# Rows of two scratch tensors in DRAM widened to multiples of 64 bytes: token list places of 64 bytes, x rows of 1600 bytes

## Chip, cores and metric

One core of a Trainium2 chip runs the whole kernel. The metric is the device time of one execution in microseconds (us). The output is one float32 tensor of 3072 x 384.

## What is computed

A delta-rule attention, then a router that sends each token to one of 8 experts, then that expert's two matrix products:

```python
# attention: B, H, S, D = 4, 8, 768, 48, all float32
k_n = k / (norm(k) + 1e-06)
for t in range(S):
    y[:, :, t] = q[:, :, t] @ state
    v_old = state^T k_n[:, :, t]
    state = state + beta[t] * outer(k_n[:, :, t], v[:, :, t] - v_old)
# bridge: x is y as 3072 tokens (N = B*S) of 384 numbers (H*D)
logits = cosine(x, expert_emb) / tau          # 8 experts
expert_idx = argmax(logits); gate_w = softmax(logits)[expert_idx]
for e in range(E):
    mask = expert_idx == e
    h = relu(x[mask] @ w1[e])                 # 384 -> 1024
    out[mask] = gate_w[mask] * (h @ w2[e])    # 1024 -> 384
```

## The kernel before

**Attention.** The sequence is cut into 12 chunks of 64 steps, and a *unit* is one chunk of two of the four batches, so there are 24 units, taken in order. A unit is loaded by SP (`load`, L112 to L127: q, k and v, rows of 192 bytes), prepared on POOL and VectorE (`prep1` to `prep3`, L294 to L310), and goes through a chain of small matrix products on TensorE (L286 is the helper `mm` that issues nearly all of them) with evictions on ScalarE and VectorE. `PLAN` (L568) gives every step of a unit a place in time; the steps of all units are sorted by it, and that order is what PE, DVE, ACT and POOL run. SP's DMAs are placed by the scheduler.

**Lists of tokens.** `outputs` (L441) writes a unit's rows of x into an SBUF tile `xc`, which holds two chunks of all four batches (256 tokens in each half, 4 units). After each second chunk, that is after every fourth unit and six times in all, the steps `route1` to `route6` (L481 to L539) pick each token's expert and its place in that expert's list. `put_on_lists` (L544) then issues four indirect DMAs from POOL (L551), called *puts* here: each scatters 128 token numbers to 128 places of `idmap`, a tensor in DRAM that has 3072 places for each of 8 experts and 3968 more behind them. Tokens of one expert get places that follow each other, so their numbers lie next to each other, 4 bytes each. `route6` writes the gate behind each row of x as its 385th number and stores the rows to `x_dram` in four DMAs by SP (L539), each of 64 partitions with two rows of 1540 bytes.

**Fill.** At the start `late_constants` (L217) fills `idmap` with the number N of a row of zeros: POOL makes a tile `none` (L254), SP stores it (L255), and SP stores the row of zeros to `x_dram` (L258).

**Experts.** From the counts of the lists 31 tiles of 128 places are laid out on one partition of VectorE (L609 to L631). `fetch` (L634) is called two tiles ahead; SP reads the expert and the place into registers, then reads the 128 places of `idmap` into `ids` (L638, only once all puts have landed), loads the expert's `w1` and `w2` (L642, L644; three buffers each), and POOL gathers the 128 rows of x by `ids` (L646). `transposed` (L651) transposes them on PE (L655), `experts` (L659) does the two products (L665, L670) and scales by the gate (L672), and POOL scatters 128 rows of 1536 bytes to the output (L673). At the start of this stage PE transposes the first two tiles before the first product.

The lines that tie the two scratch tensors together:

```python
    x_dram = tc.dram_tile([N + 1, Dm + 1], F32, name="x_dram")           # L76
    idmap = tc.dram_tile([NMAP, 1], I32, name="idmap")                   # L77
        none = ac.tile([128, NMAP // 128], I32, name="none")             # L253
        nc.gpsimd.iota(none, pattern=[[0, NMAP // 128]], base=N, channel_multiplier=0)
                out=idmap[:, :], out_offset=bass.IndirectOffsetOnAxis(ap=K["slot_i"][:, g:g + 1], axis=0),
                in_=K["tokid"][:, c - 1 + g // NU, g % NU:g % NU + 1], in_offset=None)
        ids = mk.tile([128, 1], I32, name="ids", tag="ids", bufs=5)      # L637
        read = nc.sync.dma_start(ids, idmap[bass.ds(s, T), :])           # L638
```

Of the kernel before, what the change touches and what calls it, by code (L numbers as in the profile page):

```python
# [8 lines left out]
F32 = mybir.dt.float32  # L9
I32 = mybir.dt.int32  # L10
# [12 lines left out]
def kernel(  # L23
# [37 lines left out]
    nc = tc.nc  # L61
    B, H, S, D = q.shape
    NC, NP, Dm, N = S // C, H // 2, H * D, B * S
    NU = B // 2
# [2 lines left out]
    NT = N // T + E - 1  # L67
    NMAP = E * N + NT * T

    cpool = ctx.enter_context(tc.tile_pool(name="const", bufs=1))  # L70
    att = ExitStack()
    ps = att.enter_context(tc.tile_pool(name="ps", bufs=1, space=bass.MemoryType.PSUM))
    run = cpool.tile([1, E], F32, name="run")
    base_e = cpool.tile([1, E], F32, name="base_e")
    K = {}
    x_dram = tc.dram_tile([N + 1, Dm + 1], F32, name="x_dram")  # L76
    idmap = tc.dram_tile([NMAP, 1], I32, name="idmap")  # L77

    def bank(shape):
        return ps.tile(shape, F32, name="bank", tag="bank", bufs=2)  # L80
# [15 lines left out]
    ac = att.enter_context(tc.tile_pool(name="ac", bufs=1))  # L96
    io = att.enter_context(tc.tile_pool(name="io", bufs=2))
# [35 lines left out]
    for u in range(NU):  # L133
        for i in range(2):
            nc.scalar.dma_start(out=bt[u * H:(u + 1) * H, :, i],
                                in_=beta[2 * u + i].rearrange("h (c t) -> h c t", t=C))
# [35 lines left out]
    def filled(name, bufs, value):  # L172

        ts = []
        for i in range(bufs):
            t = ac.tile(jc, F32, name=f"{name}{i}")
            nc.scalar.activation(t.rearrange("p j r c -> p (j r) c"), id64.broadcast_to(hc), ACT.Copy, scale=value)
            ts.append(t)
        return ts
# [28 lines left out]
    sqb = sqb.rearrange("p c (u h) -> p c u h", u=NU)  # L208

    PP = {s: filled(f"P{s}_", 2, 1.0) for s in LEVELS}  # L210
    S_u = []
    for u in range(NU):
        t = ac.tile([128, NP, 2, D], F32, name=f"S{u}")
# [3 lines left out]
    def late_constants():  # L217

        c = {}
        for name, value in (("second", ALU.is_ge), ("first", ALU.is_lt)):  # L220

            c[name] = ac.tile([128, 1], F32, name=name)
            nc.vector.tensor_single_scalar(c[name], trow_f[:, 0:1], float(C // 2), op=value)
        nc.vector.reciprocal(rtau, rtau)
        c["ones"] = ac.tile([128, 128], F32, name="ones")
        nc.vector.memset(c["ones"], 1.0)
        c["mask_su"] = ac.tile([128, 128], F32, name="mask_su")
        nc.gpsimd.memset(c["mask_su"], 1.0)
        nc.gpsimd.affine_select(out=c["mask_su"], in_=c["mask_su"], compare_op=ALU.is_ge, fill=0.0, base=-1,
                                pattern=[[1, 128]], channel_multiplier=-1)  # L230
        iota_ei = ac.tile([128, E], I32, name="iota_ei")
        nc.gpsimd.iota(iota_ei, pattern=[[1, E]], base=0, channel_multiplier=0)
        iota_e = ac.tile([128, E], F32, name="iota_e")
        nc.vector.tensor_copy(iota_e, iota_ei)
        c["pref_e"] = ac.tile([128, 1, E], F32, name="pref_e")
        nc.vector.tensor_scalar(c["pref_e"][:, 0, :], iota_e, -1.0, float(E), op0=ALU.mult, op1=ALU.add)
        nc.vector.tensor_scalar_mul(base_e, iota_e[0:1], float(N))
        nc.vector.tensor_copy(run, base_e)

        prow_f = ac.tile([128, 1], F32, name="prow_f")  # L240
        nc.vector.tensor_copy(prow_f, prow[:, 0:1])
        nc.vector.tensor_single_scalar(prow_f, prow_f, float(C), op=ALU.is_ge)
        nc.vector.scalar_tensor_tensor(out=prow_f, in0=prow_f, scalar=float(S), in1=trow_f[:, 0:1],
                                       op0=ALU.mult, op1=ALU.add)
        tok_i = ac.tile([128, NC, NU], I32, name="tok_i")
        nc.gpsimd.iota(tok_i, pattern=[[C, NC], [2 * S, NU]], base=0, channel_multiplier=0)
        tok_f = ac.tile([128, NC, NU], F32, name="tok_f")
        nc.vector.tensor_copy(tok_f, tok_i)
        nc.vector.tensor_scalar(tok_f, tok_f, prow_f, None, op0=ALU.add)
        c["tokid"] = ac.tile([128, NC, NU], I32, name="tokid")  # L250
        nc.vector.tensor_copy(c["tokid"], tok_f)

        none = ac.tile([128, NMAP // 128], I32, name="none")  # L253
        nc.gpsimd.iota(none, pattern=[[0, NMAP // 128]], base=N, channel_multiplier=0)  # L254
        nc.sync.dma_start(idmap.rearrange("(p n) o -> p (n o)", p=128), none)  # L255
        zrow = ac.tile([1, Dm + 1], F32, name="zrow")
        nc.vector.memset(zrow, 0.0)
        nc.sync.dma_start(x_dram[N:N + 1, :], zrow)  # L258
        K.update(c)
# [23 lines left out]
    outs = {}  # L283
# [80 lines left out]
    def product(lhsT, rhs):  # L364

        p = pair([NP, C])
        for j in range(NP):
            for a in range(2):
                for b in range(2):
                    mm(p[HALF[b], a, j], lhsT[HALF[a], j, b], rhs[HALF[a], j, b])  # L370
        return p.rearrange("p a j c -> p j a c")

    def level(U, s, by):
        p = product(U["A"][by], U["T"])
        U["P"] = PP[s][U["n"] % 2]
        nc.vector.copy_predicated(U["P"], below[s].broadcast_to(jc), p)  # L376
# [32 lines left out]
    def apply(lhsT, rhs):  # L409
        p = bank([128, H, D])  # L410
        for h in range(H):
            for i in range(2):
                mm(p[HALF[i], h], lhsT[HALF[i], h // 2, h % 2], rhs[HALF[i], h])
        return p
# [26 lines left out]
    def outputs(U):  # L441
        c, u = U["c"], U["u"]
        if u == 0 and c % 2 == 0:
            outs[c // 2] = (io.tile([128, 2, NU, Dm + 1], F32, name="xc", tag="xc"),
                            wk.tile([128, 2, NU], F32, name="ssx", tag="ssx"),
                            wk.tile([128, 2, NU, E], F32, name="lz", tag="lz"))
        xc, ssx, _ = outs[c // 2]
        p = apply(U["M"], U["Z"])
        U["x"] = xc[:, c % 2, u, 0:Dm]
        xh = U["x"].rearrange("p (h d) -> p h d", h=H)  # L450
        if c > 0:
            nc.vector.tensor_tensor(xh, p, U["Yq"], op=ALU.add)
        else:
            nc.vector.tensor_copy(xh, p)
        ysq = wk.tile([128, Dm], F32, name="ysq", tag="ysq", bufs=1)
        nc.scalar.activation(ysq, U["x"], ACT.Square, accum_out=ssx[:, c % 2, u:u + 1])
# [21 lines left out]
    def last_of_two_chunks(f):  # L478
        return lambda U: f(U["c"], *outs[U["c"] // 2]) if U["n"] % G == G - 1 else None
# [64 lines left out]
    def put_on_lists(g):  # L544

        def step(c, xc, ssx, lz):
            if g > 0:
                nc.gpsimd.memset(gap, 0.0)  # L550
            put = nc.gpsimd.indirect_dma_start(  # L551
                out=idmap[:, :], out_offset=bass.IndirectOffsetOnAxis(ap=K["slot_i"][:, g:g + 1], axis=0),
                in_=K["tokid"][:, c - 1 + g // NU, g % NU:g % NU + 1], in_offset=None)
            if g == 0:
                for other in lists[-G:]:
                    tc.add_manual_dep(put.ins, other.name, AFTER, reason="tokens' lists: two chunks after two others")
            else:
                tc.declare_no_dep(put.ins, group=f"lists{c}", reason="tokens' lists: distinct places")
            tc.add_to_no_dep_group(f"lists{c}", put.ins)
            lists.append(put.ins)  # L560
        return last_of_two_chunks(step)
# [31 lines left out]
    mk = ctx.enter_context(tc.tile_pool(name="mk", bufs=2))  # L593
# [40 lines left out]
    def fetch(i):  # L634
        e = nc.values_load(info[0:1, 0, i:i + 1], engines=(SP,), min_val=0, max_val=E - 1)
        s = nc.values_load(info[0:1, 1, i:i + 1], engines=(SP,), min_val=0, max_val=NMAP - T)
        ids = mk.tile([128, 1], I32, name="ids", tag="ids", bufs=5)  # L637
        read = nc.sync.dma_start(ids, idmap[bass.ds(s, T), :])  # L638
        for put in lists[-G:]:
            tc.add_manual_dep(read.ins, put.name, AFTER, reason="tokens' lists are complete")  # L640
        w1 = wt.tile([128, KC, F], F32, name="w1", tag="w1")
        nc.sync.dma_start(w1, moe_w1[bass.ds(e, 1)].rearrange("o (c p) f -> p (o c) f", p=128))  # L642
        w2 = wt.tile([128, NF, Dm], F32, name="w2", tag="w2")
        nc.sync.dma_start(w2, moe_w2[bass.ds(e, 1)].rearrange("o (f p) m -> p (o f) m", p=128))  # L644
        x = mk.tile([128, Dm + 1], F32, name="xg", tag="xg", bufs=5)
        nc.gpsimd.indirect_dma_start(  # L646
            out=x, out_offset=None, in_=x_dram[:, :],
            in_offset=bass.IndirectOffsetOnAxis(ap=ids[:, 0:1], axis=0))
        return ids, w1, w2, x
# [9 lines left out]
    def experts(xT, ids, w1, w2, x):  # L659
# [9 lines left out]
        for f in range(NF):  # L669
# [5 lines left out]
            in_=y, in_offset=None, bounds_check=N - 1, oob_is_err=False)  # L675

    ahead = [fetch(0), fetch(1)]
    xT = transposed(ahead[0][-1])
    for i in range(NT):
# [36 lines left out]
```

## Time and profile before

| | |
|---|---|
| three runs | 879.0, 879.75 (median), 882.95 us |
| the profiled execution | 880.7 us, of which the span of the trace is 879.0 |
| PE busy | 743.8 us (85%), 15196 instructions |
| DVE, ACT, POOL busy | 279.5, 245.3, 226.1 us |
| DMA queue of SP | 128738 packets, 116.55 MB, 46.8% of 16 engines |
| DMA queue of POOL (the indirect DMAs) | 4736 packets, 10.85 MB, 3.3% |
| instruction queue | 119 packets, 1.95 MB, 1.0% |
| granted TensorE clock, whole span | 0.94 of full speed |

All rows are from one execution; times are from the start of its span, on which the attention lies up to about 495 us, the layout of the tiles and the first fetches up to about 530, and the experts behind that. PEld is the weight load of TensorE. A bracket such as `[2.72 <-issue]` behind a row says how long the engine was idle before that row and what ended the wait; `issue` means that the engine waited for nothing that the profile shows. A "q" behind an engine's name (SPq) is its sequencer.

### The profile page before, as it was taken

How to read it: one execution, taken by the hardware profiler on the slowest of the kernel's cores; microseconds unless marked ns; L12 is line 12 of the kernel's file. 1: busy time of each engine (PE TensorE's matmuls, PEld its weight loads, DVE VectorE, ACT ScalarE, POOL GpSimd, SP SyncE). 2: the span in 40 equal slices, each digit the busy share in tenths (PEclk: the TensorE clock that was granted, in tenths of full speed). 3: DMA queues.
4: the chain of work that ended last, by engine and by line, in shares of the span. 5: the costliest groups of instructions: out<-in, count | busy, mean ns of one | idle time of the engine just before them, and what ended most of it. 6: DMA issues, size and time to landing. Idle time of an engine off the chain costs nothing. (4 is left out here: it accounts for less than half of the span.)

```text
span 879.0 us, 33263 instructions
## 1 busy us (share of the span) xinstructions
PE 743.8 (85%) x15196; PEld 636.6 (72%) x15196; DVE 279.5 (32%) x627; ACT 245.3 (28%) x468; POOL 226.1 (26%) x258
## 2 busy tenths in 40 slices
PE   1589899699789979979978308999999999999995
PEld 1478888588778868868867307777777777777774
DVE  5355556356445545534533300000000000010000
ACT  4155445254344535434523101111111111111110
POOL 3544234242423432342210201111111111111110
PEclk9999999899899999989978558999999999999998
DMA  4432112521611241040001369999999999999940
GB/s 86 77 58 56 34 35 38 56 53 35 66 31 36 50 60 33 13 48 4 4 3 40 35 242 363 329 324 321 327 326 315 328 328 328 309 323 317 329 140 0
DMA packets 134189, 129.63 MB, mean 147 GB/s; under 512 B 84538, under 2 KB 119521, under 8 KB 134050
## 3 DMA queue, kind: packets, MB, share of 16 engines
q1 hardware_dynamic: 128738, 116.55, 46.8%
q0 software_dynamic: 4736, 10.85, 3.3%
q8 instruction: 119, 1.95, 1.0%
q14 instruction: 20, 0.16, 0.1%
q10 hardware_dynamic: 576, 0.11, 0.1%
HBM read 117.91 MB, written 10.95 MB: 147 GB/s over the span
## 5 line engine op out<-in xcount | busy, mean ns | idle before, releaser
L665 PE MATMUL acc<-xTm,w 128*128 128x128 f32 x1488 | 172.9, 277 | 0.0
L665 PEld LDWEIGHTS acc<-xTm,w 128*128 128x128 f32 x1488 | 170.5, 194 | 0.3
L670 PE MATMUL acc<-w,hT 128*128 128x384 f32 x496 | 165.1, 486 | 0.0
L670 PEld LDWEIGHTS acc<-w,hT 128*128 128x128 f32 x496 | 91.9, 190 | 57.5
L667 ACT ACTIVATE hT<-acc 128x512 f32<-128x512 f32 x62 | 37.0, 597 | 331.0 <-PE acc L665 331.0
L672 DVE TENSOR_SCALAR y<-acc,xg 128x384 f32<-128x384 f32 x31 | 19.2, 618 | 305.0 <-PE acc L670 305.0
L673 POOL DMA_INDIRECT out_dram<-y,ids x31 | 31.6, 1018 | 270.1 <-DVE y L672 270.1
L286 PE MATMUL pair<-W,P 64*64 64x64 f32 x3072 | 78.5, 231 | 18.4 <-issue 14.1
L376 DVE COPY_PREDICATED P<-below,pair 128x512 f32<-128x512 int32 x96 | 70.7, 737 | 68.7 <-PE pair L286 54.4
L362 ACT ACTIVATE W<-pair 128x512 f32<-128x512 f32 x96 | 57.5, 599 | 111.2 <-PE pair L286 99.7
L301 POOL TENSOR_TENSOR rn<-rn,half 128x8 f32<-128x8 f32 x24 | 39.5, 1644 | 177.5 <-DVE rn L300 143.7
L286 PEld LDWEIGHTS pair<-W,P 64*64 64x64 f32 x3072 | 67.3, 143 | 22.6 <-issue 17.5
L286 PE MATMUL bank<-Z,G 64*64 64x48 f32 x1536 | 62.1, 232 | 13.4 <-issue 12.1
L286 PEld LDWEIGHTS bank<-Z,G 64*64 64x64 f32 x1536 | 57.0, 149 | 14.5 <-issue 12.3
L286 PE MATMUL bank<-R,W 64*64 64x48 f32 x1536 | 58.8, 225 | 8.5 <-issue 6.5
L286 PEld LDWEIGHTS bank<-R,W 64*64 64x64 f32 x1536 | 54.2, 142 | 10.1 <-issue 9.3
L286 PE MATMUL pair<-T,AJ 64*64 64x64 f32 x1536 | 42.9, 237 | 10.5 <-issue 7.7
L346 PE MATMUL bank<-ident,W 128*128 128x128 f32 x288 | 48.8, 293 | 1.2 <-ACT W L362 0.9
L655 PE MATMUL acc<-ident,xg 128*128 128x128 f32 x93 | 16.0, 283 | 35.0 <-DMA xg<-x_dram,ids 35.0
L655 PEld LDWEIGHTS acc<-ident,xg 128*128 128x128 f32 x93 | 12.3, 145 | 44.9 <-issue 31.7
L286 PEld LDWEIGHTS pair<-T,AJ 64*64 64x64 f32 x1536 | 34.9, 145 | 12.5 <-issue 8.9
L340 POOL TENSOR_TENSOR G<-G,upper 128x512 f32<-128x512 f32 x24 | 30.7, 1279 | 37.5 <-ACT G L334 36.1
(160 smaller groups left out, 881.5 us busy)
## 6 DMA issues: line engine op xcount, KB each, us to landing
w<-in_moe_w_dram SPq DMA_DIRECT2D x62, 1536.0 KB
x_dram<-xc SPq DMA_DIRECT2D x24, 192.5 KB
k_in<-in_k_dram SPq DMA_DIRECT2D x48, 96.0 KB
QQ<-in_q_dram SPq DMA_DIRECT2D x48, 96.0 KB
v_in<-in_v_dram SPq DMA_DIRECT2D x48, 96.0 KB
ids<-idmap SPq DMA_DIRECT2D x31, 0.5 KB
xg<-x_dram,ids POOLq DMA_INDIRECT x31
out_dram<-y,ids POOLq DMA_INDIRECT x31
```

What stands on the lines that cost most here:

```text
L286: nc.tensor.matmul(out_, lhsT=lhsT, rhs=rhs, start=start, stop=True, skip_group_check=True)
L301: nc.gpsimd.tensor_tensor(out=U["rn"], in0=U["rn"], in1=half[:, 0], op=ALU.pow)
L340: nc.gpsimd.tensor_tensor(M, M, upper.broadcast_to(hc), op=ALU.mult)
L346: nc.tensor.transpose(p[:, j].rearrange("p r c -> p (r c)"), src[:, j].rearrange("p r c -> p (r c)"), ident)
L362: nc.scalar.activation(out_, in_, ACT.Copy)
L376: nc.vector.copy_predicated(U["P"], below[s].broadcast_to(jc), p)
L655: nc.tensor.transpose(psX[:, j, :], x[:, j * 128:(j + 1) * 128], ident)
L665: nc.tensor.matmul(psH[:, i, :], lhsT=w1[:, j, (f + i) * 128:(f + i + 1) * 128], rhs=xT[:, j, :], start=(j == 0), stop=(j == KC - 1))
L667: nc.scalar.activation(hT[:, f:f + 4, :], psH, ACT.Relu)
L670: nc.tensor.matmul(psO, lhsT=hT[:, f, :], rhs=w2[:, f, :], start=(f == 0), stop=(f == NF - 1))
L672: nc.vector.tensor_scalar_mul(y, psO, x[:, Dm:Dm + 1])
L673: nc.gpsimd.indirect_dma_start(out=out[:, :], out_offset=bass.IndirectOffsetOnAxis(ap=ids[:, 0:1], axis=0), in_=y, in_offset=None, bounds_ ...
```

## The change

A place of `idmap` becomes 16 numbers, 64 bytes, and a put writes 16 copies of the token's number to it; `tokid` holds the copies, and the fill and the reads of `ids` carry 16 times the bytes. A row of `x_dram` becomes 400 numbers, 1600 bytes (384 of x, the gate, 15 zeros). Since only the first 385 are written by the computation, the zeros are set once in two tiles `XC` that are used in turn in place of the pool's two buffers. The fill is made by a memset where it was an iota.

```diff
+    ROW, ID = Dm + 16, 16
...
-    x_dram = tc.dram_tile([N + 1, Dm + 1], F32, name="x_dram")
-    idmap = tc.dram_tile([NMAP, 1], I32, name="idmap")
+    x_dram = tc.dram_tile([N + 1, ROW], F32, name="x_dram")
+    idmap = tc.dram_tile([NMAP, ID], I32, name="idmap")
...
+    XC = []
+    for i in range(2):
+        XC.append(ac.tile([128, 2, NU, ROW], F32, name=f"XC{i}"))
+        nc.gpsimd.memset(XC[i][:, :, :, Dm:], 0.0)
...
-        c["tokid"] = ac.tile([128, NC, NU], I32, name="tokid")
-        nc.vector.tensor_copy(c["tokid"], tok_f)
-
-        none = ac.tile([128, NMAP // 128], I32, name="none")
-        nc.gpsimd.iota(none, pattern=[[0, NMAP // 128]], base=N, channel_multiplier=0)
+        c["tokid"] = ac.tile([128, NC, NU, ID], I32, name="tokid")
+        nc.vector.tensor_copy(c["tokid"], tok_f.unsqueeze(3).broadcast_to([128, NC, NU, ID]))
+
+        none = ac.tile([128, NMAP // 128 * ID], I32, name="none")
+        nc.gpsimd.memset(none, N)
         nc.sync.dma_start(idmap.rearrange("(p n) o -> p (n o)", p=128), none)
-        zrow = ac.tile([1, Dm + 1], F32, name="zrow")
+        zrow = ac.tile([1, ROW], F32, name="zrow")
...
-            outs[c // 2] = (io.tile([128, 2, NU, Dm + 1], F32, name="xc", tag="xc"),
+            outs[c // 2] = (XC[c // 2 % 2],
...
-                in_=K["tokid"][:, c - 1 + g // NU, g % NU:g % NU + 1], in_offset=None)
+                in_=K["tokid"][:, c - 1 + g // NU, g % NU], in_offset=None)
...
-        ids = mk.tile([128, 1], I32, name="ids", tag="ids", bufs=5)
+        ids = mk.tile([128, ID], I32, name="ids", tag="ids", bufs=5)
...
-        x = mk.tile([128, Dm + 1], F32, name="xg", tag="xg", bufs=5)
+        x = mk.tile([128, ROW], F32, name="xg", tag="xg", bufs=5)
```

The order of PE, DVE and ACT stays as it was. POOL has the two small memsets of `XC` more among its first ones, and an instruction of another size at the fill. This is POOL before, at the fill (`Ksq`, `rn` and `KK_109` prepare the second unit, `ess` belongs to the experts' embeddings):

```order
L246 IOTA tok_i 128x24
L254 IOTA none 128x223
L296 TENSOR_TENSOR Ksq<-k_in 128x384
L301 TENSOR_TENSOR rn<-rn,half 128x8
L310 TENSOR_TENSOR KK_109<-k_in,rn 128x8x48
L268 TENSOR_TENSOR ess<-ess,half 8x1
```

and this is POOL now, with everything in the same order behind a memset of 3568 numbers per partition:

```order
L252 IOTA tok_i 128x24
L260 MEMSET none 128x3568
L302 TENSOR_TENSOR Ksq<-k_in 128x384
L307 TENSOR_TENSOR rn<-rn,half 128x8
L316 TENSOR_TENSOR KK_109<-k_in,rn 128x8x48
L274 TENSOR_TENSOR ess<-ess,half 8x1
```

On SP, before, the fill stands between the two halves of the fourth unit's q:

```order
L116 DMA QQ_84<-in_q_dram 64x8x48
L255 DMA idmap<-none 128x223
L116 DMA QQ_84<-in_q_dram 64x8x48
L258 DMA x_dram<-zrow 1x385
L116 DMA v_in<-in_v_dram 64x8x48 x2
L116 DMA k_in<-in_k_dram 64x8x48 x2
```

and now it stands two DMAs later, behind the row of zeros, with the loads of the second unit's v and of the fifth unit's k right behind it:

```order
L118 DMA QQ_84<-in_q_dram 64x8x48 x2
L264 DMA x_dram<-zrow 1x400
L261 DMA idmap<-none 128x3568
L118 DMA v_in<-in_v_dram 64x8x48 x2
L118 DMA k_in<-in_k_dram 64x8x48 x2
```

## Rows read from the trace of the kernel before

**Rows 1.** Experts' stretch: length; busy (instructions) of PE, PEld, DVE, ACT, POOL; PEclk, DMA, GB/s.

```profile
556.00:860.00 304.00, 303.00 (x1869) 242.04 (x1869) 29.89 (x55) 33.44 (x56) 53.99 (x55) 1.00 0.91 307
```

**Rows 2.** The scatters to the output: the page's groups (busy, mean ns, idle before).

```profile
L673 POOL DMA_INDIRECT out_dram<-y,ids x31 | 31.6, 1018 | 270.1 <-DVE y L672 270.1
```

**Rows 3.** The same view, each stretch one unit, from one L423 to a next.

```profile
144.06:170.12 26.06, 17.38 (x567) 15.47 (x569) 9.70 (x24) 9.50 (x18) 9.73 (x12) 0.91 0.53 56
170.12:186.71 16.59, 15.81 (x564) 14.51 (x561) 8.92 (x17) 8.22 (x16) 5.36 (x5) 0.94 0.20 40
186.71:203.27 16.56, 15.27 (x555) 13.74 (x545) 8.88 (x17) 8.21 (x16) 5.32 (x5) 1.00 0.20 40
203.27:221.58 18.31, 16.96 (x576) 15.47 (x578) 10.92 (x26) 8.22 (x16) 6.29 (x6) 1.00 0.19 37
221.58:247.60 26.02, 18.82 (x567) 17.45 (x563) 9.83 (x24) 8.22 (x17) 9.60 (x12) 0.80 0.53 56
...
297.61:320.63 23.02, 17.15 (x564) 15.47 (x560) 9.82 (x24) 8.55 (x17) 9.54 (x12) 0.93 0.47 63
...
371.91:397.12 25.21, 19.33 (x561) 17.56 (x557) 9.64 (x23) 8.40 (x17) 9.59 (x12) 0.80 0.36 42
```

**Rows 4.** Timeline around the first four puts: start, us, engine, line, operation, [idle before].

```profile
155.60 1.01 POOL L551 DMA_INDIRECT idmap<-tokid,slot_i  x1 [0.17 <-issue]
...
159.70 0.26 PE L286 MATMUL bank<-Z,G 64*64 64x48 f32 x3 [2.72 <-issue]
...
163.92 0.38 PE L286 MATMUL pair<-W,P 64*64 64x64 f32 x3 [1.68 <-issue]
167.22 0.51 PE L286 MATMUL pair<-W,P 64*64 64x64 f32 x6 [2.92 <-issue]
```

**Rows 5.** Timeline around the fifth four puts, after the last load of the attention.

```profile
450.86 0.96 POOL L551 DMA_INDIRECT idmap<-tokid,slot_i  x1 [0.22 <-issue]
...
454.84 0.22 PE L286 MATMUL bank<-enT,xT 128*64 128x8 f32 x1 [1.36 <-issue]
...
462.00 0.56 PE L286 MATMUL bank<-R,W 64*64 64x48 f32 x5 [4.50 <-issue]
```

**Rows 6.** By stretch: the end of that wait, and the four stores of x behind it.

```profile
457.50:462.00 4.50, 0.00 (x0) 0.00 (x0) 0.00 (x0) 0.00 (x0) 0.00 (x0) 0.50 0.00 0
...
464.00:468.50 4.50, 4.50 (x123) 4.05 (x117) 1.98 (x3) 1.02 (x2) 0.00 (x0) 0.50 0.72 183
```

**Rows 7.** Timeline, from the last put to the first read of a list.

```profile
499.69 0.96 POOL L551 DMA_INDIRECT idmap<-tokid,slot_i  x1 [0.22 <-issue]
...
511.38 0.39 SPq L638 DMA_DIRECT2D ids<-idmap  x1
```

**Rows 8.** SP's waits: us in total, times, longest.

```profile
SPq L638 <- DMA idmap<-tokid,slot_i: 7.7, 1, 7.7
```

**Rows 9.** SP's instructions of the line that reads the lists.

```profile
L638 SPq EVENT_SEMAPHORE  x35: 27/28/28, 510.7 to 827.8; - x35
L638 SPq ALU_OP  x31: 32/33/53, 502.9 to 827.7; - x31
```

**Rows 10.** POOL's groups up to 25 us: busy us, mean ns of one, idle before.

```profile
L214 POOL MEMSET S<- 128x384 f32 x2 | 0.8, 407 | 0.0
...
L254 POOL IOTA none<- 128x223 int32 x1 | 0.3, 333 | 0.0
...
L228 POOL MEMSET mask_su<- 128x128 f32 x1 | 0.2, 206 | 0.0
```

**Rows 11.** Timeline at the start: from the fill to the first unit's products.

```profile
19.70 0.33 POOL L254 IOTA none<- 128x223 int32 x1
...
20.01 0.82 POOL L296 TENSOR_TENSOR Ksq<-k_in 128x384 f32<-128x384 f32 x1
...
22.18 0.48 DVE L300 TENSOR_REDUCE rn<-Ksq 128x8 f32<-128x384 f32 x1
...
22.64 1.28 SPq L116 DMA_DIRECT2D v_in<-in_v_dram  x2
...
29.09 1.32 PE L286 MATMUL pair<-KT 48*64 48x128 f32 x17
...
46.40 0.83 POOL L314 TENSOR_TENSOR v_in<-v_in,sqb 128x384 f32<-128x384 f32 x1
```

## The prediction
> **What bounds the kernel now.** I read the table by stretches first, then the timeline at the places where a stretch is longer than its neighbours, then SP's waits at the seam between attention and experts. While the experts run, PE is busy in 303.00 of 304.00 us at the full clock [rows 1]; nothing that the change does to lists or rows of x is waited for there, so this part keeps its length and only its start can move. In the attention the work of one unit is some 560 matmuls. Three units in a row take 16.59, 16.56 and 18.31 us for 564, 555 and 576 of them, 17.15 in the mean, but every fourth unit takes 23 to 26 us for the same number [rows 3]. It is always the unit in which POOL issues four puts. What is lost there is in the timeline: PE stands still for 2.72, 1.68 and 2.92 us, and each of these waits is put down to "issue": no engine, no tile, no DMA of data that the profile shows [rows 4]. That looks like PE waiting for its own instructions, which come by DMA through the same 16 engines; the profile does not name it, so this stays an inference.
>
> What blocks the DMA engines is told by the fifth four puts, because there they are alone: no load of the attention is left, and the stores of x come later. Still PE stops for 1.36 and then 4.50 us [rows 5]. In the whole of the second stop every engine is idle and the DMA share is 0.00 [rows 6]: nothing is being moved, something is being waited out. It ends at 462.00, 11.1 us after the last of these puts was issued at 450.86. Around the first four puts the last stop ends at 167.22, 11.6 us after the last put, issued at 155.60 [rows 4]. And at the end of the attention SP, which waits for the puts by name, comes free at 510.7 [rows 9], 11.0 us after the last put at 499.69 [rows 7]. Three places, the same 11 us. So **the 4-byte scatters need some 11 us to be finished in DRAM, and other DMAs are held up meanwhile**.
>
> The stores of x are not what hurts. Behind the fifth four puts they run by themselves at 183 GB/s, and PE is busy in 4.50 of 4.50 us beside them [rows 6], with rows of 1540 bytes. And 31 scatters of 128 whole rows of 1536 bytes to the output [rows 2] run beside the experts with PE never waiting [rows 1], so neither an indirect DMA nor a row at a scattered address is slow as such. What only the puts have is that they write 4 bytes, and that tokens of one expert write right beside each other.
>
> **The change part by part.** *Puts of 64 bytes, each place its own 64 bytes.* No instruction is added: still 24 indirect DMAs of 128 descriptors. I take it that a put then behaves like the scatters to the output and holds up nothing. Units one to four of those with puts take 26.06, 26.02, 23.02 and 25.21 us [rows 3]; with the calm 17.15 each, 8.91 + 8.87 + 5.87 + 8.06 = 31.7 us go, the half clock after the stops (0.80 to 0.93 granted in these stretches) among them. At the fifth, where the pipeline runs out and no calm unit stands beside it, I count the two stops alone, 1.36 + 4.50 = 5.9 us [rows 5]. Together 37.6 us. The other bound is 0: no row shows a scatter of 64 bytes. I take the full gain: the nearest row, the scatter of 1536 bytes, costs PE nothing, and like it the new put gives each token a place that it shares with no other.
>
> *The seam.* SP has its registers for the first tile and waits 7.7 us for the puts [rows 8]; its first instruction on that line stands at 502.9 and the wait ends at 510.7 [rows 9]. If the last put lands within some 3 us of its issue at 499.69, the read of the first list goes out 7.7 us earlier than 511.38 [rows 7], and SP's own work is next. The gather, the transposes and the experts are chained to that read and move with it. Bounds 0 and 7.7; I take 7.7.
>
> *Rows of 1600 bytes.* 4% more bytes for stores that hide behind PE [rows 6] and gathers that hide behind the experts [rows 1]: 0. If that cover were gone, 1600 for 1540 bytes in 4.5 us of stores is 0.2 us each.
>
> *The fill.* POOL makes 3568 numbers per partition where it made 223. Memsets of 128 and 384 numbers take 206 and 407 ns, so 0.79 ns for each further one: 0.407 + 3184 x 0.00079 = 2.9 us, against 0.333 [rows 10]; in proportion to 384 it would be 3.8. The `Ksq` behind it then ends near 23.4 instead of 20.83, and the reduction on VectorE that starts at 22.18 must wait for it: 1.25 us late, with the copies of `tokid` in the shadow. From there POOL and VectorE hand the preparation to and fro until PE starts the first unit's products at 29.09 [rows 11], with no slack that I would count on: **1.3 us lost**, at most 2.1. The two memsets of 16 numbers per row stand before the first `Ksq`, which waits for its load: 0.
>
> The 1.83 MB of the fill (128 x 3568 x 4 bytes) now run in SP's queue ahead of the loads from 22.64 on. At the rate of the stores of x, 183 GB/s [rows 6], that is 10 us at most; the v that stands right behind it is used by POOL at 46.40 [rows 11], 23.8 us after its issue. Hidden. The reads of `ids` carry 8 KB instead of 512 bytes: 0, beside 3 MB of weights per tile.
>
> **Sum.** 880.7 (the profiled execution) - 37.6 - 7.7 + 1.3 = 836.7 us. The median of the runs is 0.95 below the profiled one, so 835.8: I say **836**. The range of this case: down to 826, with the four units as short as the shortest neighbour, 4 x (17.15 - 16.56) = 2.4, the fifth losing 7.9 like the mean of the four instead of 5.9, the fill hidden, 1.3, and up to 4 us of the work after the fifth puts, which runs at half clock [rows 6]; up to 850, if a third of the 45.3 us stays.
>
> **A rule against it.** The Trainium skill, in "DMA: Bandwidth & Descriptors", Specifications, asks for at least 512 bytes per transfer for full rate and says that below this the engine does a read-modify-write. By that rule puts of 64 bytes stay what puts of 4 bytes are. The trace agrees in so far as rows of 1536 and 1540 bytes do not stall; no row here shows a write between the 4 bytes of the puts and the 892 per partition (223 numbers) of the fill.
>
> **The rivals.** *The stall stays, because 64 bytes are still a small write.* For it: no row shows a write of this size, and the puts keep their number. Against it: stalling 11 us for 512 writes while the engines show a share of 0.00 looks like writes queueing for one place, not like a cost of each. Then only what the four stretches lose more than the fifth could go with aligned rows of x, 31.7 - 4 x 5.9 = 8.1 us at most, and 0 at least: 880.7 - (0 to 8.1) + 1.3 = 874 to 882. Chance 0.13; that is the rule's case too.
>
> *Half of it goes.* Each place is alone in its 64 bytes, but every write still costs a part of its wait: 22.7 of the 45.3 us remain, 880.7 - 22.7 + 1.3 = 859. Chance 0.06.
>
> *Slower.* The memory may charge by the separate 64-byte lines that a put touches. Now 16 neighbours share a line; then each of the 128 writes has its own, and 16 times the bytes. The place is the same: the stops after the puts and SP's wait. It decides as soon as a put needs longer than today's 11 us; at twice that, the 45.3 us come once more, 880.7 + 45.3 + 1.3 = 927. Against it speaks that the scatter to the output touches 24 lines for each row and holds up nothing [rows 1, 2]. Chance 0.05, with the case that the fill outlasts its 23.8 us of cover.
>
> **How the numbers follow.** The forecast has 0.76, the rivals 0.13, 0.06 and 0.05. The range must hold 8 in 10: the forecast's own 826 to 850, and up to 864 for the half. A measurement of this kernel tells 0.5%, 4.4 us, from no change. Faster by more: 0.76 + 0.06, and 0.03 of the rival whose times begin at 874: 0.85. The same: 0.09. Slower: 0.06.
>
> **What would show it.** In the profile after, units with puts should take 16 to 19 us like their neighbours, the waits of PE for "issue" behind the puts should be gone, the clock should stay at 1.00 through the attention, and SP's wait for the puts should fall from 7.7 us to below 1. The experts should still take 303 us of PE time in 304, only earlier. PE's first products should start near 30.4. It is wrong if a stop of several us still ends some 11 us after the fourth put, or if the stops are gone but the stretches stay long, or if the v of the second unit is waited for at its scaling.

## The result and the profile after

The change makes the kernel faster: **846.07 us** (843.09 to 847.93) against 879.61 us (879.0 to 882.95), four runs each, ratio **0.9608** (95%: 0.9569 to 0.9647). In two later sets of runs, on the second and the third chip of the table below, the same kernel came to 0.9527 (0.9478 to 0.9575) and 0.9542 (0.9498 to 0.9587). The forecast was 836, within a range of 826 to 850; the time lies in the range, 10 us above the forecast. The profiled execution took 847.12 us, with a span of 845.1 against 879.0: 33.9 us to account for. Line numbers after L217 stand six higher now: the puts are L557, the reads of `ids` L644, the fill L260, `mm` L292.

The stretches of the profile after, cut like those of [rows 3], and the experts', columns as in [rows 1]. The first four are the first four units in which puts are issued, the fifth holds the fifth four puts, and the row behind it is the next unit:

```profile
147.43:166.72 19.29, 17.68 (x572) 16.04 (x574) 9.66 (x24) 9.40 (x18) 9.75 (x12) 0.91 0.35 79
217.59:234.89 17.30, 15.82 (x567) 14.04 (x563) 9.62 (x23) 8.22 (x17) 9.61 (x12) 1.00 0.38 87
285.54:303.66 18.12, 16.18 (x564) 14.27 (x560) 9.66 (x23) 8.32 (x17) 9.61 (x12) 1.00 0.37 84
353.93:370.99 17.06, 15.69 (x564) 14.00 (x560) 9.66 (x24) 8.22 (x17) 9.60 (x12) 1.00 0.28 66
404.92:429.27 24.35, 20.60 (x563) 18.84 (x559) 9.89 (x22) 7.34 (x14) 6.27 (x9) 0.81 0.02 5
...
429.27:445.93 16.66, 16.30 (x453) 14.92 (x450) 6.84 (x17) 5.07 (x11) 0.00 (x0) 0.66 0.21 53
...
528.00:824.00 296.00, 296.00 (x1820) 236.09 (x1819) 29.18 (x54) 32.25 (x54) 52.82 (x53) 1.00 0.92 312
```

The four units now take 19.29, 17.30, 18.12 and 17.06 us where [rows 3] have 26.06, 26.02, 23.02 and 25.21: 28.5 us less in all. The fifth has not become calm: 24.35 us at a granted TensorE clock of 0.81, and 16.66 us behind it at 0.66. The experts are what they were, PE busy throughout.

The seam, from the timeline, as in [rows 7]:

```profile
474.05 0.96 POOL L557 DMA_INDIRECT idmap<-tokid,slot_i  x1 [0.22 <-issue]
...
478.06 0.38 SPq L644 DMA_DIRECT2D ids<-idmap  x1
```

From the last put to the first read of a list it is 4.01 us instead of 11.69, and SP's waits no longer have a row for the puts where [rows 8] had 7.7. The trace after also has the landing of the new puts: 2.1 to 4.0 us after their issue, 3.0 in the median of the 24.

The start, from the timeline, as in [rows 11]:

```profile
20.14 3.15 DVE L240 CAST iota_e<-iota_ei 128x8 f32<-128x8 int32 x1 [1.23 <-POOL iota_ei L238]
20.19 3.08 POOL L260 MEMSET none<- 128x3568 int32 x1
...
23.23 0.83 POOL L302 TENSOR_TENSOR Ksq<-k_in 128x384 f32<-128x384 f32 x1
...
25.55 0.39 DVE L263 MEMSET zrow<- 1x400 f32 x1
25.88 0.48 DVE L306 TENSOR_REDUCE rn<-Ksq 128x8 f32<-128x384 f32 x1
...
32.78 1.99 PE L292 MATMUL pair<-KT 48*64 48x128 f32 x32
```

The fill takes 3.08 us, and a VectorE cast of 8 numbers per partition beside it takes 3.15 us. VectorE's row of small instructions behind that cast ends with `zrow`, and only then comes the reduction that the second unit waits for, at 25.88 instead of 22.18. PE's first products start 3.7 us later than in [rows 11].

**The account**, after less before: four units -28.5; the fifth with the one behind it, from 19.76 + 22.67 = 42.43 us to 24.35 + 16.66 = 41.01, -1.4; the seam -7.7; the start +3.7. Together -33.9, as much as the spans differ. That it comes out to the tenth is chance: of the start's 3.7 us, 2.6 are left at the mark of the first unit (the instruction by which [rows 3] cut the units, at 65.11 against 62.49), and the stretches not listed here, each within 1.1 us of what it was, make up the rest.

### The profile page after: what moved, and what is told of

It reads as the page before. It is cut to its first block, busy times and chain, and to the rows that moved or that the text cites. A ratio compares the mean times of both kernels' runs of the same rounds, so it can differ in the third digit from the quotient of the medians.

```text
span 845.1 us, 33265 instructions
## 1 busy us (share of the span) xinstructions
PE 739.0 (87%) x15196; PEld 630.8 (75%) x15196; DVE 282.4 (33%) x627; ACT 245.0 (29%) x468; POOL 229.5 (27%) x260
## 3 DMA queue, kind: packets, MB, share of 16 engines
q8 instruction: 119, 1.95, 1.0%
## 5 line engine op out<-in xcount | busy, mean ns | idle before, releaser
L292 PE MATMUL pair<-W,P 64*64 64x64 f32 x3072 | 76.8, 226 | 10.5 <-issue 6.8
L292 PEld LDWEIGHTS pair<-W,P 64*64 64x64 f32 x3072 | 65.9, 138 | 14.4 <-issue 9.3
L292 PE MATMUL bank<-R,W 64*64 64x48 f32 x1536 | 59.6, 224 | 7.7 <-issue 5.4
L292 PE MATMUL bank<-Z,G 64*64 64x48 f32 x1536 | 58.2, 224 | 7.6 <-issue 6.3
L292 PEld LDWEIGHTS bank<-R,W 64*64 64x64 f32 x1536 | 54.0, 140 | 10.3 <-issue 9.6
L292 PEld LDWEIGHTS bank<-Z,G 64*64 64x64 f32 x1536 | 52.9, 140 | 8.7 <-issue 6.7
L292 PE MATMUL pair<-T,AJ 64*64 64x64 f32 x1536 | 40.7, 228 | 6.4 <-issue 3.4
L292 PEld LDWEIGHTS pair<-T,AJ 64*64 64x64 f32 x1536 | 32.8, 136 | 8.6 <-issue 4.8
```

The lines of the kernel that those rows point to most:

```text
L292: nc.tensor.matmul(out_, lhsT=lhsT, rhs=rhs, start=start, stop=True, skip_group_check=True)
```

## Experiments

Theory: what stalls is many writes to places that lie beside each other in the same few bytes of DRAM. Rivals: the size of a write is what counts; the aligned rows of x carry the gain; the new fill gives part of it back.

| kernel | median (us) | ratio to before | 95% |
|---|---|---|---|
| first chip, before: 875.2 | | | |
| e1_lists_only | 831.58 | 0.951 | 0.9432 to 0.9587 |
| e2_rows_only | 882.95 | 1.011 | 1.0072 to 1.0148 |
| e3_pitch_only | 829.88 | 0.9498 | 0.9437 to 0.9558 |
| e4_small_fill | 826.23 | 0.9448 | 0.9378 to 0.9518 |
| second chip, before: 881.36 | | | |
| after_again | 841.12 | 0.9527 | 0.9478 to 0.9575 |
| e5_32bytes | 839.9 | 0.9513 | 0.9465 to 0.9561 |
| e6_8bytes | 877.47 | 0.9944 | 0.9903 to 0.9984 |
| e7_last_puts_only | 834.99 | 0.9466 | 0.9405 to 0.9526 |
| third chip, before: 875.77 | | | |
| after_third | 834.57 | 0.9542 | 0.9498 to 0.9587 |
| e1_again | 831.86 | 0.9518 | 0.9469 to 0.9568 |
| e8_spread | 834.46 | 0.9533 | 0.9487 to 0.9578 |
| e9_best | 834.24 | 0.9524 | 0.9478 to 0.957 |

All edits are made in the changed kernel. The times expected of e1 to e4 were set by the 846.07 above; on the first chip of this table the kernel before is some 4 us faster and the whole change was not run, so these four are read by their ratios and traces.

### Lists alone, rows alone

```diff
-    ROW, ID = Dm + 16, 16
+    ROW, ID = Dm + 1, 16      # e1_lists_only
+    ROW, ID = Dm + 16, 1      # e2_rows_only
```

> The change with the rows of x left at 1540 bytes: only the places of the lists are 64 bytes. If the puts alone held up the DMA engines, the time is that of the change, 844 to 849 us, with units that have puts at 16 to 19 us. If the unaligned rows of x have a share of their own, it lies above: 855 us or more, with PE standing still again for issue in units with puts.

> The other half: rows of x of 1600 bytes, places of the lists of 4 bytes as before. If the puts alone held up the DMA engines, nothing is gained, 874 to 882 us, the read of the first list still goes out some 11 us after the last put, and only the start is as early as before (first products of PE near 29 us). If the rows of x matter, 850 to 870 us.

With the lists alone the gain is whole, 0.951. With the rows alone there is none: 1.011, even 1.1% slower, which I cannot explain. Two stretches of e2 with puts, and SP's wait:

```profile
144.70:170.05 25.35, 18.17 (x571) 16.90 (x574) 9.80 (x23) 9.50 (x18) 9.72 (x12) 0.87 0.47 59
222.28:248.31 26.03, 19.18 (x567) 17.32 (x563) 9.80 (x23) 8.22 (x17) 9.60 (x12) 0.87 0.43 57
```

```profile
SPq L644 <- DMA idmap<-tokid,slot_i: 8.6, 1, 8.6
```

These are the stretches of [rows 3] and the wait of [rows 8] over again. On the third chip e1 once more, beside the whole change:

> The lists alone, on the chip of the anchor. If the rows of 1600 bytes bring nothing, the same as the anchor within 2 us. If they help, this is slower by up to 8 us, the most that the four units with puts lost more than the fifth in the kernel before.

831.86 against 834.57, with intervals that overlap: the rows of 1600 bytes bring no gain that can be measured here.

### Size or neighbours

In e3 a put writes 4 bytes, as before the change, but its places stay 64 bytes apart.

```diff
-        nc.vector.tensor_copy(K["slot_i"], slot)
+        nc.vector.tensor_scalar_mul(K["slot_i"], slot, float(ID))
...
-                out=idmap[:, :], out_offset=...,
-                in_=K["tokid"][:, c - 1 + g // NU, g % NU], in_offset=None)
+                out=idmap.rearrange("n (o i) -> (n o) i", i=1), out_offset=...,
+                in_=K["tokid"][:, c - 1 + g // NU, g % NU, 0:1], in_offset=None)
```

> Places at a pitch of 64 bytes, but a put writes only the first number, 4 bytes (the index is multiplied by 16 in the instruction that made it a whole number; fill and reads as in the change). If the stall comes from neighbours that write into the same 64 bytes, it is gone: 844 to 849 us. If any write below 64 bytes is slow by itself, it is back: 872 to 884 us, with SP waiting for the puts some 7 us. Anything between says that both count.

829.88 us, ratio 0.9498: the whole gain. The five stretches of e3 that hold puts:

```profile
148.57:165.17 16.60, 15.24 (x572) 13.87 (x574) 9.66 (x24) 9.40 (x18) 9.72 (x12) 1.00 0.41 90
215.52:232.75 17.23, 15.59 (x567) 13.96 (x563) 9.70 (x23) 8.21 (x17) 9.60 (x12) 1.00 0.39 86
283.05:300.08 17.03, 15.23 (x564) 13.74 (x560) 9.74 (x23) 8.31 (x17) 9.58 (x12) 1.00 0.39 87
350.25:366.59 16.34, 15.21 (x564) 13.80 (x560) 9.78 (x24) 8.22 (x17) 9.58 (x12) 1.00 0.26 67
398.62:415.82 17.20, 15.86 (x568) 14.51 (x564) 9.83 (x22) 7.23 (x14) 3.66 (x5) 1.00 0.02 5
```

All are as long as calm units, at the full clock. Since the writes are the 4 bytes of before, their size is not the cause; that they lie further apart is what cures them. This is the experiment that separates the theory from the first rival.

The traces also show that it is other DMAs that are held up, which the prediction had only argued. These are two stretches of the kernel before, behind the first four puts (the last one at 155.60):

```profile
160.00:164.00 4.00, 2.32 (x117) 2.10 (x108) 1.23 (x2) 1.20 (x3) 0.00 (x0) 1.00 1.03 29
164.00:168.50 4.50, 1.39 (x25) 1.10 (x24) 0.73 (x1) 0.04 (x1) 0.00 (x0) 0.65 0.04 4
```

In the first, the DMA engines are taken all the time (share 1.03) and move 29 GB/s; in the second almost nothing moves, as behind the fifth puts [rows 6]. In e3, whose last put there stands at 159.79, the first of these stretches has a share of 0.48 at 88 GB/s. The queues tell whose time it is: from 140 to 170 us the packets of SP's queue, loads and stores, take 44.2% of the 16 engines for 1.38 MB in the kernel before and 23.5% for 1.54 MB in e3, while the puts' own packets take 0.3% in both.

### How far apart

```diff
-    ROW, ID = Dm + 16, 16
+    ROW, ID = Dm + 16, 8      # e5_32bytes
+    ROW, ID = Dm + 16, 2      # e6_8bytes
```

> Places of 32 bytes, 8 copies: two neighbours share 64 bytes. If a write waits for the other writes to its 64 bytes, a chain is 2 instead of 16 long: nearly all of the gain, and the fill is half as long, so the same time as the change or up to 2 us less. If a write has to be 64 whole bytes to be fast, several us of stops come back at each four puts, 855 us or more.

> Places of 8 bytes, 2 copies: 8 neighbours share 64 bytes. If the stall grows with the neighbours in 64 bytes, half of the 11 us from the last put to the read of the first list remains beyond the some 3 us without stall, 6 to 7 us, and SP waits 1 to 4 us for the puts; the time lies between the change and the kernel before. If any neighbour is enough, SP waits 7 us again and the time is that of the kernel before.

> The change itself, unaltered, so that the parts stand against it on one chip and the fifth four puts are seen a second time. If the slow unit at the fifth puts in its first profile (24.35 us, with short waits of PE for issue and the clock at 0.81) belongs to the change, it is there again and the time is some 12 us above that of the lists alone. If it was one execution's, the stretch is 17 us like in the kernels with part of the change, and the time lies within some 3 us of theirs.

32 bytes do as well as 64: 839.9 against 841.12. With 8 bytes almost all is lost again, 877.47. The first three stretches with puts of e6, then its wait at the seam:

```profile
143.10:171.62 28.52, 21.29 (x571) 18.77 (x574) 9.80 (x23) 9.61 (x18) 9.72 (x12) 0.76 0.44 52
224.24:247.30 23.06, 19.27 (x571) 17.28 (x563) 9.82 (x23) 8.21 (x17) 9.58 (x12) 0.85 0.46 64
296.22:319.29 23.07, 17.18 (x565) 14.90 (x560) 9.68 (x23) 8.32 (x17) 9.58 (x12) 1.00 0.53 64
```

```profile
SPq L644 <- DMA idmap<-tokid,slot_i: 7.5, 1, 7.5
```

Half as many neighbours in 64 bytes do not mean half the stall: of the two outcomes named for e6 it is the second, that any neighbour is enough; the wait is 7.5 where [rows 8] have 7.7. The step from bad to good lies between 8 and 32 bytes. With 32 bytes, two places still share 64: so either what must not be shared is 32 bytes or less, or two writers of 64 bytes do no harm yet. The runs do not tell these apart. Nor do they tell places that share a few bytes from places that are merely close together: the experiments change the pitch alone, and with it how wide a put spreads over DRAM. Only that a put at a pitch of 8 bytes, spread twice as wide as before, is hardly better speaks for sharing. The Trainium skill, in "Collectives: The Full Stack", Rules for kernel authors, has the buffers of collectives aligned to 32 bytes, because that prevents a read-modify-write in hardware; e5 and e6 agree with that edge (839.9 and 877.47). But the rows of x of 1540 bytes, aligned to 4 bytes only, cost nothing in e1, so misalignment by itself is not enough for a stall.

### The fill

```diff
-        none = ac.tile([128, NMAP // 128 * ID], I32, name="none")
+        none = ac.tile([128, 32 * ID], I32, name="none")
...
-        nc.sync.dma_start(idmap.rearrange("(p n) o -> p (n o)", p=128), none)
+        places = idmap.rearrange("(p n) o -> p (n o)", p=128)
+        for a in range(0, NMAP // 128 * ID, 32 * ID):
+            n = min(32 * ID, NMAP // 128 * ID - a)
+            nc.sync.dma_start(places[:, a:a + n], none[:, 0:n])
```

> The change with the fill made from a tile of 512 numbers per partition instead of 3568, stored by seven DMAs. POOL's memset falls from 3.08 us to some 0.5, VectorE's cast beside it from 3.15 us to below 0.6, and the first products of PE start near 29.6 us instead of 32.78. If that delay goes through to the end, 842 to 844 us; if the attention makes up for it later, 845 to 848 us.

The timeline of e4 at the start:

```profile
19.59 0.61 DVE L240 CAST iota_e<-iota_ei 128x8 f32<-128x8 int32 x1 [1.22 <-POOL iota_ei L238]
19.64 0.53 POOL L260 MEMSET none<- 128x512 int32 x1
...
22.78 0.48 DVE L309 TENSOR_REDUCE rn<-Ksq 128x8 f32<-128x384 f32 x1
...
29.68 1.99 PE L295 MATMUL pair<-KT 48*64 48x128 f32 x32
```

The memset shrinks from 3.08 to 0.53 us, the cast beside it from 3.15 to 0.61, and PE's first products come at 29.68 instead of 32.78. So the cast is as long as the memset, and 3.1 of the 3.7 us at the start are the memset's doing. The median, 826.23, is the lowest of the set, but its interval overlaps those of e1 and e3, and the whole change was not run on this chip. A version with this fill, the old rows of x and one more edit (e8's, below) was to bring all together:

> The small fill, the lists of 64 bytes, rows of x of 1540 bytes as before, and the fifth puts set apart. If each does what was seen or is expected of it alone, the anchor less some 3 us for the fill and up to 6 us for the puts: 832 to 838 us beside an anchor of 841. If the rows of 1600 bytes are worth something, it is above that.

It missed. Its first products stand at 29.48, those of the whole change on the same chip at 32.26, and the times are 834.24 and 834.57: 2.8 us gained at the start did not show at the end. The marks of the units show where they go: the lead is 3.5 us at the first (61.87 against 65.36) and 0.4 at the sixth (146.33 against 146.77), ahead of the first puts. What takes it back there is open; in e4 it is not taken back (62.58 against e1's 65.74 at the first mark, 437.61 against 441.95 at the last). No version is shown to beat the change.

### The fifth four puts

```diff
         def step(c, xc, ssx, lz):
+            if c < NC - 1:
+                return
             if g > 0:
```

e7 leaves out the first five of the six groups of four puts, so those tokens are on no list and their output is missing; the last group and the work of the experts stay.

> The change with the first five of the six times four puts left out: those tokens stay out of the lists, so the output lacks them, while the counts, the tiles and all other work are the same. If puts of 64 bytes hold up nothing, the attention takes as long as with them, less than 3 us of difference in all. If they still cost something, up to 2 us for each of the five, 5 to 10 us less.

The fifth unit in e7, then in the unaltered change on the same chip, then on the third chip:

```profile
403.83:421.08 17.25, 15.78 (x565) 14.56 (x561) 9.86 (x23) 7.34 (x14) 2.07 (x2) 1.00 0.02 5
```

```profile
406.22:430.36 24.14, 20.32 (x562) 17.92 (x558) 9.87 (x22) 7.34 (x14) 6.28 (x9) 0.83 0.02 5
```

```profile
398.87:416.22 17.35, 15.88 (x568) 14.67 (x564) 9.88 (x22) 7.34 (x14) 3.67 (x5) 1.00 0.02 5
```

Without the early puts the kernel takes 834.99 against 841.12 on that chip. That is 6 us in the medians, with intervals that overlap; in the profiled executions the fifth unit and the stretch behind it (24.14 + 14.18 us against 17.25 + 13.11) differ by 8.0. The unaltered change thus has its slow fifth unit a second time there, as had been asked of after_again, but not on the third chip, where the unit and the 12.77 us behind it are calm with all puts.

The other traces say the same: with places 32 bytes or more apart the fifth unit is slow in all three profiles of the first set and of the second chip (24.35, 24.14, and 23.63 in e5) and calm, 17.2 to 17.4 us, in all seven of the first and third chips (e1 twice, e3, e4, after_third, e8, e9). It may differ between executions too: of the four runs of after_again the profiled one is the slowest, 845.8 us at a clock of 0.954 over its span, and the others have 839.2 to 841.84 us at 0.964 to 0.966.

How PE loses the time: against the calm unit of the third chip it is busy 20.60 us instead of 15.88, with part of its matmuls at half clock, and idle 2.3 us longer. The waits are in the timeline of the first profile after, around the fifth puts (421.75 to 425.65):

```profile
423.79 0.35 PE L292 MATMUL pair<-W,P 64*64 64x64 f32 x5 [0.25 <-issue]
424.55 0.35 PE L292 MATMUL pair<-W,P 64*64 64x64 f32 x5 [0.40 <-issue]
425.28 0.35 PE L292 MATMUL pair<-W,P 64*64 64x64 f32 x5 [0.39 <-issue]
...
427.49 1.53 PE L292 MATMUL bank<-Z,G 64*64 64x48 f32 x24 [1.11 <-issue]
```

PE gets five matmuls, waits 0.4 us, gets five more. Over the same time, in stretches of 1 us (the last three columns are clock, DMA share and GB/s):

```profile
409.00:410.00 1.00, 1.00 (x46) 1.00 (x43) 0.88 (x3) 0.03 (x1) 0.00 (x0) 1.00 0.09 16
...
412.00:413.00 1.00, 1.00 (x38) 0.93 (x33) 0.93 (x2) 0.64 (x2) 0.88 (x1) 1.00 0.07 16
...
416.00:417.00 1.00, 1.00 (x9) 1.00 (x10) 0.52 (x2) 0.34 (x1) 0.00 (x0) 0.90 0.00 0
417.00:418.00 1.00, 1.00 (x16) 0.98 (x16) 0.00 (x0) 0.00 (x0) 0.00 (x0) 0.50 0.06 16
...
423.00:424.00 1.00, 0.75 (x15) 0.55 (x11) 0.00 (x0) 0.00 (x0) 0.88 (x1) 0.69 0.10 24
424.00:425.00 1.00, 0.49 (x10) 0.20 (x5) 0.00 (x0) 0.00 (x0) 0.78 (x3) 1.00 0.05 9
425.00:426.00 1.00, 0.35 (x5) 0.23 (x5) 0.67 (x1) 0.00 (x0) 0.78 (x3) 1.00 0.05 6
426.00:427.00 1.00, 0.33 (x4) 0.35 (x5) 0.05 (x1) 0.00 (x0) 0.61 (x1) 1.00 0.02 3
427.00:428.00 1.00, 0.51 (x11) 0.50 (x12) 0.00 (x0) 0.26 (x1) 0.00 (x0) 0.52 0.04 8
```

The clock fell from 1.00 to 0.50, from 2.4 to 1.2 GHz, at about 416.8 (0.90 in the mean of that microsecond, 0.50 in the next), some 5 us before the first put of the group, so its fall is not the doing of these puts. Nor is it the change's: the kernel before has the same fall ahead of its fifth puts (the first one at 446.96):

```profile
441.00:442.00 1.00, 1.00 (x9) 0.98 (x9) 0.66 (x2) 0.47 (x1) 0.00 (x0) 0.92 0.00 0
442.00:443.00 1.00, 1.00 (x11) 0.97 (x13) 0.00 (x0) 0.00 (x0) 0.00 (x0) 0.50 0.05 16
```

Before the fall PE stood still for most of a microsecond (busy 0.25 from 414 to 415, in the kernel before 0.00 from 439 to 440) and was then busy again; on the third chip it was busy 0.40 from 408 to 409 and the clock stayed at 1.00, on the second 0.65 from 416 to 417 and the clock fell. No rule for the fall comes out of this. To try the puts themselves, e8 puts a memset of 128 x 2048 numbers between those of the fifth group, to spread them:

```diff
+    rest = ac.tile([128, 2048], F32, name="rest")
...
-                nc.gpsimd.memset(gap, 0.0)
+                nc.gpsimd.memset(rest if c == NC - 3 else gap, 0.0)
```

> The change once more, as the anchor for the three others on this chip. The unit at the fifth puts takes 24 us if the short waits of PE belong to the kernel, 17 us if they come and go with the chip or the execution.

> The change, with the fifth four puts set apart by a memset of 2048 numbers per partition between them, some 1.6 us more each. If the waits of PE there come from four puts one right behind the other, the unit falls from 24 to 17 or 18 us and the time by some 6 us against the anchor. If they have another cause, or are not there on this chip, the time is the anchor's within 2 us.

Inconclusive: on that chip the fifth unit took 17.35 us without the edit and 17.34 with it, so there was nothing to cure. What joins puts, clock and trickle at the fifth unit stays open; only that it comes and goes is shown.

## Why the prediction was right or wrong

**The cause: right, and shown as far as the pitch goes.** The prediction took the stall for writes queueing for one place in DRAM, not for a cost of each small write. e3 shows it: 4-byte writes 64 bytes apart gain as much as the change. e6 shows that eight neighbours in 64 bytes stall nearly like sixteen, e5 that a pitch of 32 bytes is enough. That what the neighbours share is one place, and not only a region, is still argued.

**Four units, -31.7 forecast, -28.5 measured.** The mechanism was right. The size was off by 3.2 us, because the new units are 17.9 us in the mean (71.77 / 4) where the calm 17.15 was taken. The first, 19.29 at a clock of 0.91, makes 2.1 of it. In e3 the same four take 67.2 us, less than 4 x 17.15 = 68.6, so the step itself can be whole.

**The fifth, -5.9 forecast, -1.4 measured.** This is the term that was most mis-sized. The two long waits of [rows 5] did go, and the stretch in which they lay went from 22.67 to 16.66 us, 6.0 less. What the term left out is the unit ahead of it, which went from 19.76 to 24.35 us, 4.6 more: PE is idle 2.7 us longer in it, in a trickle of waits of 0.25 to 1.11 us, and busy 1.9 us longer, with matmuls at half clock before and behind the trickle. By the prediction's own sign, stops gone and a stretch still long, its account fails for this unit. The prediction's sentence that the clock should stay at 1.00 through the attention was wrong here (0.81 and 0.66) and in the first of the four (0.91). After_third shows the term come true, and more: 17.35 + 12.77 = 30.1 us for the two stretches, against 42.43 in the profile before (the chips may differ).

**The seam, -7.7 forecast, -7.7 measured.** The estimate of a landing "within some 3 us" holds: the traces have 3.0 us in the median (at most 4.0), 3.1 in e3 and 2.9 in e5. SP's first instruction on the line stands some 3.2 us after the last put in both kernels (502.9 and 477.3), so 7.7 us was all that could go.

**The fill, +1.3 forecast, +3.7 measured.** The memset itself was sized well: 2.9 us forecast, 3.08 measured, and `Ksq` ends at 24.06 where 23.4 was forecast. The step that failed is "with the copies of `tokid` in the shadow": VectorE was taken to run its small instructions beside the memset, but its cast lasted for the memset's whole length and the instructions behind it came after. The reduction then waited for VectorE, not for `Ksq`. The kernel before had a row that could have warned of it, beside POOL's `Ksq` (20.01 to 20.83 in [rows 11]):

```profile
20.11 0.74 DVE L238 COPY run<-base_e 1x8 f32<-1x8 f32 x1
```

It copies eight numbers in 0.74 us and ends as `Ksq` does; after the change, with nothing on POOL beside it, the same copy takes 0.16 us. The Trainium skill, in "SBUF — State Buffer", SBUF: two separate sides and its part Who interferes with whom, says that VectorE and GpSimd share a pair of ports that the instruction which starts first holds for its whole length, and that a cast can be one that wants it. The trace agrees in so far as the cast took 0.61 us beside a memset of 0.53 and 3.15 beside 3.08. It took 0.17 beside the old fill, an iota of 0.33 that ran on, so that one did not hold it; and in the rows the cast starts 0.05 us ahead of the memset and still ends with it, which the order of the starts does not explain.

**Rows of 1600 bytes, 0 forecast: no gain, right.** e1 has the full gain without them, on two chips. Whether they cost something is not settled: e2 was 1.1% slower than the kernel before.

**The fill's DMA, hidden: right.** It goes out at 26.38, and the scaling of the v behind it starts at 49.22 where [rows 11] have 46.40, 2.8 us later and so no more than the start itself; it never waits for a load. In e3, which has the same fill, it lands 6.5 us after its issue, against the "10 us at most".

**The rivals.** "64 bytes are still a small write" falls with the result, and e3 shows that a small write alone does not stall. The rule that stood beside it, the Trainium skill's "DMA: Bandwidth & Descriptors", Specifications, of a read-modify-write below 512 bytes, does not explain the stall: e3's 4-byte writes are far below that and do not stall. "Half of it goes", 859 us, falls by its time and by its mechanism: what was left sat mostly in one place, the fifth unit, not in every put. "Slower, by separate lines" falls: each put touches 128 separate pieces now and lands sooner, 3.0 us after its issue in the median.

Of the profiled execution 44.0 us were to go and 33.9 went; the miss of 10.1 us is 3.2 + 4.5 + 2.4. On the second and third chips the medians gain 40.2 and 41.2 us.

**What stays inference.** That PE waits for its own instructions is not shown by an experiment. Two things speak for it. First, SP's loads and stores are slowed beside the puts, as shown above. Second, the table of DMA queues on the profile's page has

```profile
q8 instruction: 119, 1.95, 1.0%
```

which is 1.95 MB / 119 = 16.4 KB a packet, and in the 1 us stretches above, where nothing else is moving, 16 GB/s for one microsecond come back every three to five microseconds: the same 16 KB. In the trickle, from 421 to 428, the stretches carry 50 KB in all; the four puts are 32.8 KB of that (4 x 128 x 64 bytes), which by this estimate leaves room for about one such packet in 7 us.

## What to carry to other kernels

Small scattered writes that land side by side in DRAM, 4 or 8 bytes apart, can hold up other DMAs, here for some 11 us after each group of 512; give each place 32 bytes of its own before looking for a faster scatter (16 was not tried), and pad the pitch, since at a pitch of 64 bytes 4 bytes written did as well as 64. When PE idles on "issue" while the DMA share is near zero, or near one with little moved (29 GB/s here), look for such writes in the 10 us before. And size a new GpSimd instruction on a start path by what VectorE does at the same time, not by GpSimd alone.

## What had not been expected of the hardware

- Places of 8 bytes are nearly as bad as places of 4 (877.47 against 881.36 on one chip), places of 32 as good as 64 (839.9 against 841.12).
- A cast of 8 numbers per partition on VectorE took 3.15 us beside a GpSimd memset of 3.08, and 0.17 in the kernel before.
- The same kernel has its fifth unit at 24.35, 24.14 and 17.35 us in three profiles, with the granted clock at 0.81, 0.83 and 1.00 in it.
- Beside puts of 4-byte places the packets of SP's queue took nearly twice the engine time (44.2% against 23.5%) for fewer bytes, while the puts' own packets took 0.3% either way.
- The rows of x aligned to 64 bytes, alone, made the kernel 1.1% slower (0.7 to 1.5%); no row read here says why.
